# Top-k attention and SwiGLU FFN on one core: the order of V, scores and transposes on TensorE

## The chip, the cores and the metric

The kernel runs on one core of a Trainium2 chip. The metric is the time of one execution on the device in microseconds, as the median of several runs. The text names five engines as the profile does: PE (TensorE, matrix products and transposes; PEld is its loading of weights), DVE (VectorE), ACT (ScalarE), POOL (GpSimd) and SP (SyncE, which issues most DMAs).

## The reference

The inputs q, k and v have the shape 8 x 8 x 576 x 64 (batch, heads, sequence, head dimension), all in float32. Attention keeps for each query the 32 largest scores and gives all others no weight:

```python
scores = scale * np.matmul(q, k.transpose(0, 1, 3, 2))
kth = np.partition(scores, -top_k, axis=-1)[..., -top_k:-top_k + 1]
scores = np.where(scores >= kth, scores, -1000000000.0)
scores = scores - np.max(scores, axis=-1, keepdims=True)
attn = np.exp(scores)
attn = attn / (np.sum(attn, axis=-1, keepdims=True) + 1e-09)
x = np.matmul(attn, v)            # then (B,H,S,D) -> (B*S, H*D)
g = x @ w_gate                    # 512 x 1536
silu = g * (1.0 / (1.0 + np.exp(-g)))
out = (silu * (x @ w_val)) @ w_out   # 1536 x 512
```

There are 4608 tokens of 512 numbers after the attention.

## The kernel before

Heads are worked in pairs. A unit is one batch, one piece of the queries and one pair of heads. There are 160 units, counted n: for each of the 8 batches, four pieces of 128 queries (a full unit: two heads, 1152 scores a partition) and one last piece of 64 queries (a half unit, with both heads on the 128 partitions: 576 scores), for each of the four pairs. The four half units of a batch come together, at n mod 20 = 16 to 19.

The main loop (its body starts with `for n in range(NU + VALUES)`) is a pipeline that an iteration writes out by hand, and the order of writing is the order on each engine: at the end the kernel ties every instruction to the one before it on its engine. In iteration n stand, each for its own unit:

- `select(n)` on DVE: four rounds of MAX8 (L329) with MATCH_REPLACE8 (L333) between them find the 32 largest scores of each row of `sc`; then L339 writes a large negative number into `e` wherever a score is below the 32nd.
- `penalize(n - 1)` on POOL: L349 makes the bias, and L351 adds `sc` to `e`. This is the last reading of that unit's `sc`.
- `weigh(n - 1)` on ACT: exp with row sums (L360), and eps (L365).
- `normalize(n - 2)`: the reciprocal on DVE (L372), then a product on ACT (L375).
- `turn(n - 3)`, the transposes: `e` is transposed on PE (L387) in groups of four, one and four blocks (four and one for a half unit), and ACT copies each group to `et` (L388).
- `finish_unit(n - 4)` with `values`, called V here: the products with v on PE (L407 and L416) into one tile `av`, and ACT's copy to the FFN's input `xT` (L431).
- `scores(n + 1)`: a generator in two steps. The first issues the products of q and k on PE, four tiles `s` for a full unit (L308) and two for a half unit (L294). The second issues ACT's copies of these tiles to `sc` (L313, L299). `next(nxt)` runs the first step; `run(nxt)` runs what is left.

Every PSUM tile of the attention, those of the transposes, V, scores and of the preparation of k and q (`prep`, L255 and L263), comes from one pool of five banks, `ps_t`, in turn; the FFN has three banks of its own, `ps_f`. `sc` has two buffers, so the scores of n + 1 go into the buffer that unit n - 1 had.

Behind the attention's block of an iteration stand the FFN's pieces. `share(n)` and `credit` set how many an iteration gets. A block of 256 tokens (18 of them) starts once all V's of its tokens are written out: products with w_gate and w_val (L471), whose results ACT takes from PSUM (L496 to L498, L503) and POOL multiplies (L499, L504), then the products with w_out in a scheme of seven quarter products instead of eight (L557), with sums on POOL (L543 to L605). ACT's and POOL's parts of the FFN are kept in two lists, `on_act` and `on_pool`, and written out by `flush` at set places of the iteration.

In the first iterations the weights are loaded and rounded piece by piece as well (`rounded`, L114 to L123); `early[0]()` pulls ACT's part of one piece forward to its place between V's copy and exp. The loads of k, q and v are issued on SP after the block in question.

Of the kernel before, what the change touches and what calls it, by code (L numbers as in the profile page):

```python
# [25 lines left out]
def kernel(  # L26
# [174 lines left out]
    def rounding(n):  # L201
        for _ in range(n):
            next(weight, None)
# [28 lines left out]
    def load_v(i):  # L232
        b, hp = pairs[i]
        h = slice(2 * hp, 2 * hp + 2)
        vt = slabs.tile([P, 2, J, D], FP32, tag="v", name="v")
        v_last = slabs.tile([R, 2, D], FP32, tag="vl", name="v_last")
        vl = vlast[i % NV]
        nc.sync.dma_start(
            vt[:].rearrange("p h j d -> p h (j d)"),
            v[b, h, 0:JP].rearrange("h (p j) d -> p h (j d)", j=J),  # L240
        )
        nc.sync.dma_start(v_last[:], v[b, h, JP:S].rearrange("h p d -> p h d"))
        for hh in range(2):
            o = hh * R
            nc.sync.dma_start(vl[o : o + R, o : o + R], v[b, 2 * hp + hh, JP:S])
        vs[i] = (vt, v_last, vl)
# [27 lines left out]
    def n_heads(qt):  # L274

        return 1 if qt == J else 2

    def scores(n):
        b, qt, hp = units[n]
        slab = preps[b * NHP + hp]  # L280
        sc = work.tile([P, 2 * S], FP32, tag="sc", name="sc", bufs=2)
        halves = [slice(0, D), slice(D, P)]
        half = S // 2

        def bank():
            return ps_t.tile([P, 512], FP32, tag="t", name="s")


        if qt == J:
            banks = [bank() for _ in range(2)]  # L290
            for i, ps in enumerate(banks):
                for d in halves:
                    k0 = R + i * half
                    nc.tensor.matmul(  # L294
                        ps[d, 0:half], slab[d, S + R : S + 2 * R], slab[d, k0 : k0 + half]
                    )
            yield
            for i, ps in enumerate(banks):
                nc.scalar.copy(sc[:, i * half : (i + 1) * half], ps[:, 0:half])  # L299
        else:  # L300
            q0 = S + 2 * R + qt * P
            banks = []
            for i in range(2):
                for hh, d in enumerate(halves):
                    ps = bank()
                    banks.append((i + 2 * hh, ps))
                    k0 = (1 - hh) * R + i * half
                    nc.tensor.matmul(  # L308
                        ps[:, 0:half], slab[d, q0 : q0 + P], slab[d, k0 : k0 + half]
                    )  # L310
            yield
            for i, ps in banks:
                nc.scalar.copy(sc[:, i * half : (i + 1) * half], ps[:, 0:half])  # L313
        state[n] = dict(sc=sc)

    def select(n):

        nh = n_heads(units[n][1])
        sc = state[n]["sc"]
        m = small.tile([P, 2, TOP_K], FP32, tag="m", name="m", bufs=2)  # L320
        heads = [slice(t * S, (t + 1) * S) for t in range(nh)]
        rest = work.tile([P, 2 * S], FP32, tag="rest", name="rest", bufs=1)
        e = work.tile([P, 2 * S], FP32, tag="e", name="e", bufs=4)
        state[n] |= dict(m=m, e=e, heads=heads)
        cur = sc
        rounds = TOP_K // 8
        for r in range(rounds):
            for t, hs in enumerate(heads):
                nc.vector.max(m[:, t, 8 * r : 8 * r + 8], cur[:, hs])  # L329
                yield  # L330
            if r < rounds - 1:
                for t, hs in enumerate(heads):
                    nc.vector.match_replace(  # L333
                        rest[:, hs], m[:, t, 8 * r : 8 * r + 8], cur[:, hs], LOWEST
                    )
                    yield
                cur = rest
        for t, hs in enumerate(heads):
            nc.vector.tensor_scalar(  # L339
                e[:, hs], sc[:, hs], m[:, t, TOP_K - 1 : TOP_K], FAR, ALU.is_lt, ALU.mult  # L340
            )
# [26 lines left out]
    def normalize(n):  # L368
        st = state[n]
        tot, e, heads = st.pop("tot"), st["e"], st.pop("heads")  # L370
        nh = len(heads)
        nc.vector.reciprocal(tot[:, 0:nh], tot[:, 0:nh])  # L372
        yield
        for t, hs in enumerate(heads):
            nc.scalar.mul(e[:, hs], e[:, hs], tot[:, t : t + 1])  # L375
# [22 lines left out]
    def values(n):  # L398

        b, qt, hp = units[n]  # L400
        vt, v_last, vl = vs[b * NHP + hp]
        et = state.pop(n)["et"]
        last = qt == J
        ql = R if last else P
        av = ps_t.tile([P, P], FP32, tag="t", name="av")
        if not last:
            nc.tensor.matmul(av[:], vl[:], et[:, J, :], start=True, stop=False)  # L407
        for c in range(J + 1 if last else J):
            kl = R if c == J else P
            for hh in range(2):  # L410
                moving = (
                    et[0:kl, c, hh * R : (hh + 1) * R]
                    if last
                    else et[:, c + hh * (J + 1), :]
                )
                nc.tensor.matmul(  # L416
                    av[hh * R : (hh + 1) * R, 0:ql],
                    v_last[:, hh, :] if c == J else vt[:, hh, c, :],
                    moving,
                    start=last and c == 0,  # L420
                    stop=c == (J if last else J - 1),
                )
        c0 = b * S + qt * P
        at = c0
        while at < c0 + ql:
            kb = at // BLK
            n_c = min((kb + 1) * BLK, c0 + ql) - at
            if kb not in xT:
                xT[kb] = ffn.tile([P, NHP, BLK], FP32, tag="xT", name="xT", bufs=3)
                done[kb] = 0  # L430
            nc.scalar.copy(  # L431
                xT[kb][:, hp, at - kb * BLK : at - kb * BLK + n_c],
                av[:, at - c0 : at - c0 + n_c],
            )
            done[kb] += n_c
            at += n_c
# [16 lines left out]
    def flush(queue):  # L453
        while queue:
            queue.pop(0)()
# [224 lines left out]
    def fetch(n):  # L680

        b, qt, hp = units[n]
        i = b * NHP + hp
        if qt == 0:
            yield from prep(i)
        if qt == J and i + NHP < len(pairs):
            load(i + NHP)
# [19 lines left out]
    def run(steps):  # L707
        for _ in steps:
            pass

    def finish_unit(n):
        values(n)
        b, qt, hp = units[n]
        if qt == J and b + 1 < B:
            load_v((b + 1) * NHP + hp)
# [11 lines left out]
    TURN, VALUES = 3, 4  # L727
    due = [2.0]
    for n in range(NU + VALUES):
        nh = n_heads(units[n][1]) if n < NU else 1  # L730
        topk = select(n) if n < NU else no
        over[n - 1] = normalize(n - 1) if 0 <= n - 1 < NU else no
        nxt = scores(n + 1) if n + 1 < NU else no
        ahead = fetch(n + 2) if n + 2 < NU else no
        norm = over.pop(n - 2, no)

        def dve(k, beside=True):

            for _ in range(k * nh):
                next(topk, None)  # L740
                due[0] += 5 / 6 if beside else 0
                if due[0] >= 1:
                    due[0] -= 1
                    rounding(1)

        if n >= NU - NHP:
            credit[0] = 8.0
        else:
            credit[0] = min(credit[0] + share(n), share(n) + 1)
        flush(on_act)  # L750
        if 0 <= n - 1 < NU:
            penalize(n - 1)
        flush(on_pool)
        if 0 <= n - TURN < NU:
            run(turn(n - TURN))
        if n >= VALUES:
            finish_unit(n - VALUES)
        next(nxt, None)

        early[0]()  # L760
        if 0 <= n - 1 < NU:
            weigh(n - 1)
        run(nxt)


        dve(2, beside=False)
        if 2 <= n + 2 < NHP:
            load(n + 2)
        if n < NHP:
            load_v(n)  # L770
        pieces(2)
        flush(on_act)
        dve(1)
        dve(1)
        next(norm, None)
        run(norm)

        flush(on_pool)
        next(ahead, None)
        pieces(1)  # L780
        next(ahead, None)
        dve(1)
        pieces(1)
        dve(2, beside=False)
        run(topk)
        pieces(6)
# [50 lines left out]
```

## Time and profile before

| | |
|---|---|
| median of 3 runs | 1821.28 us (1821.05 to 1821.64) |
| span of the profiled execution, first to last instruction | 1817.8 us |
| between this span and the median of the runs | 3.5 us |
| mean granted clock of PE | 0.967 |
| busy: PE, DVE, ACT, POOL | 1708.7, 1610.7, 1218.7, 1036.4 us |
| ACT: exp (L360), both heads | 288 x 0.777 us |
| ACT: copies of scores (L313) | 512 x 0.402 us |
| ACT: copies of transposes (L388), large ones | 288 x 0.598 us |
| POOL: addition (L351), full unit | 128 x 2.640 us |

The profiled execution's time as a whole is not listed beside its span. Times in the profile count from the start of the span. A wait is listed as the engine and line that waited, what it waited for, and the time. A matmul's row is longer than the time until the next one can start, so a busy PE is not one at its peak; PE's speed is better seen in the starts of its rows.

### The profile page before, as it was taken

How to read it: one execution, taken by the hardware profiler on the slowest of the kernel's cores; microseconds unless marked ns; L12 is line 12 of the kernel's file. 1: busy time of each engine (PE TensorE's matmuls, PEld its weight loads, DVE VectorE, ACT ScalarE, POOL GpSimd, SP SyncE). 2: the span in 40 equal slices, each digit the busy share in tenths (PEclk: the TensorE clock that was granted, in tenths of full speed). 3: DMA queues.
4: the chain of work that ended last, by engine and by line, in shares of the span. 5: the costliest groups of instructions: out<-in, count | busy, mean ns of one | idle time of the engine just before them, and what ended most of it. 6: DMA issues, size and time to landing. Idle time of an engine off the chain costs nothing.

```text
span 1817.8 us, 30526 instructions
## 1 busy us (share of the span) xinstructions
PE 1708.7 (94%) x10756; PEld 1409.2 (78%) x10756; DVE 1610.7 (89%) x3372; ACT 1218.7 (67%) x2977; POOL 1036.4 (57%) x930
## 2 busy tenths in 40 slices
PE   4458999899999899999999999999999999999999
PEld 2346778687788788887888878887888878888887
DVE  7999999999999799997999989998999989998400
ACT  6778666676667676666767676767676766675532
POOL 5788756455565645554455636564556554646354
PEclk6669999899999999999999999999999999999999
DMA  7432030002100030000300021000300011000000
GB/s 191 125 108 90 14 85 7 12 1 50 45 1 13 2 82 12 13 1 22 73 12 2 13 56 39 1 12 3 74 19 13 1 36 33 1 13 12 1 12 12
DMA packets 109305, 59.65 MB, mean 33 GB/s; under 512 B 88544, under 2 KB 96992, under 8 KB 109152
## 3 DMA queue, kind: packets, MB, share of 16 engines
q1 hardware_dynamic: 108016, 57.37, 12.1%
q8 instruction: 85, 1.39, 0.3%
q14 instruction: 68, 0.56, 0.1%
q10 hardware_dynamic: 1136, 0.33, 0.1%
HBM read 48.23 MB, written 9.44 MB: 32 GB/s over the span
## 4 chain that ended last, share of the span: by engine, by line
PE 86%; DVE 8%; ACT 2%; POOL 2%; issue 2%; DMA 0%; SPq 0%; ACTq 0%; POOLq 0%
PE f L471 41%; PE x_ps L557 9%; PE av L416 8%; PE etps L387 7%; PE s L308 7%; PE y_ps L557 7%; DVE m L329 3%; DVE rest L333 3%; PE s L294 2%; PE av L407 1%; PE o_ps L517 1%; PE kqps L263 1%; DVE size L121 1%; DVE e L339 0%; POOL p L543 0%
## 5 line engine op out<-in xcount | busy, mean ns | idle before, releaser
L329 DVE MAX8 m<-rest 128x8 f32<-128x576 f32 x864 | 612.7, 744 | 2.2
L351 POOL TENSOR_TENSOR e<-e,sc 128x1152 f32<-128x1152 f32 (+1 forms) x160 | 383.1, 2394 | 83.7 <-DVE e L339 76.3
L333 DVE MATCH_REPLACE8 rest<-m,rest 128x576 f32<-128x576 f32 x576 | 423.1, 740 | 0.0
L471 PE MATMUL f<-xT,wg 128*128 128x256 f32 x1728 | 401.6, 382 | 0.0
L471 PE MATMUL f<-xT,wv 128*128 128x256 f32 x1728 | 399.1, 382 | 0.0
L471 PEld LDWEIGHTS f<-xT,wg 128*128 128x128 f32 x1728 | 323.1, 190 | 62.6 <-issue 21.3
L471 PEld LDWEIGHTS f<-xT,wv 128*128 128x128 f32 x1728 | 324.5, 190 | 58.7 <-issue 16.6
L499 POOL TENSOR_TENSOR h<-h,half_g 128x512 f32<-128x512 f32 x108 | 138.2, 1280 | 292.7 <-ACT h L498 292.2
L329 DVE MAX8 m<-sc 128x8 f32<-128x576 f32 x288 | 205.0, 747 | 104.0 <-ACT sc L299 57.8
L388 ACT COPY et<-etps 128x512 f32<-128x512 f32 (+1 forms) x448 | 184.1, 483 | 131.0 <-PE etps L387 130.2
L360 ACT ACTIVATE e<-e,bias 128x576 f32<-128x576 f32 x288 | 222.1, 777 | 57.5 <-POOL e L351 57.2
L387 PE MATMUL etps<-ident,e 128*128 128x128 f32 (+1 forms) x1312 | 184.5, 286 | 79.3 <-POOL size L122 18.2
L504 POOL TENSOR_TENSOR h<-h,val 128x512 f32<-128x512 f32 x108 | 139.6, 1293 | 186.3 <-ACT val L503 186.1
L387 PEld LDWEIGHTS etps<-ident,e 128*128 128x128 f32 (+1 forms) x1312 | 159.6, 147 | 106.0 <-POOL size L122 20.7
L375 ACT ACTIVATE e<-e,tot 128x576 f32<-128x576 f32 x288 | 212.0, 790 | 0.9 <-DVE tot L372 0.9
L333 DVE MATCH_REPLACE8 rest<-m,sc 128x576 f32<-128x576 f32 x288 | 211.5, 740 | 0.0
L308 PE MATMUL s<-kqT 64*128 64x288 f32 x1024 | 178.8, 449 | 14.1 <-ACT kqT L268 8.3
L339 DVE TENSOR_SCALAR e<-sc,m 128x576 f32<-128x576 f32 x288 | 177.2, 651 | 3.4
L416 PE MATMUL av<-et,v 128*64 128x128 f32 (+1 forms) x2560 | 170.3, 278 | 0.0
L313 ACT COPY sc<-s 128x288 f32<-128x288 f32 x512 | 164.0, 402 | 2.9 <-PE s L308 2.9
L496 ACT ACTIVATE h<-f 128x512 f32<-128x512 f32 x108 | 65.2, 604 | 133.3 <-PE f L471 133.3
L416 PEld LDWEIGHTS av<-et,v 128*64 128x64 f32 x2560 | 134.1, 143 | 22.8 <-issue 6.8
(73 smaller groups left out, 2029.1 us busy)
## 6 DMA issues: line engine op xcount, KB each, us to landing
v<-in_v_dram SPq DMA_DIRECT2D x32, 256.0 KB, 2.9
kq_in<-in_k_dram SPq DMA_DIRECT2D x63, 128.0 KB, 2.8
kq_in<-in_q_dram SPq DMA_DIRECT2D x63, 128.0 KB, 3.0
w<-in_moe_w_gate_dram SPq DMA_DIRECT2D x12, 512.0 KB, 3.7
w<-in_moe_w_val_dram SPq DMA_DIRECT2D x12, 512.0 KB, 3.8
w<-in_moe_w_out_dram SPq DMA_DIRECT2D x12, 512.0 KB, 3.5
out_dram<-o SPq DMA_DIRECT2D x38, 128.0 KB, 2.4
out_dram<-o SPq DMA_DIRECT2D x16, 256.0 KB, 2.4
```

The costliest lines, as they stand in the source:

```text
L308: nc.tensor.matmul(ps[:, 0:half], slab[d, q0 : q0 + P], slab[d, k0 : k0 + half])
L329: nc.vector.max(m[:, t, 8 * r : 8 * r + 8], cur[:, hs])
L333: nc.vector.match_replace(rest[:, hs], m[:, t, 8 * r : 8 * r + 8], cur[:, hs], LOWEST)
L339: nc.vector.tensor_scalar(e[:, hs], sc[:, hs], m[:, t, TOP_K - 1 : TOP_K], FAR, ALU.is_lt, ALU.mult)
L351: nc.gpsimd.tensor_tensor(e[:, every], e[:, every], sc[:, every], ALU.add)
L360: nc.scalar.activation(e[:, hs], e[:, hs], AF.Exp, bias=bias[:, t : t + 1], scale=scale, accum_out=tot[:, t : t + 1],)
L375: nc.scalar.mul(e[:, hs], e[:, hs], tot[:, t : t + 1])
L387: nc.tensor.transpose(ps[0:kl, c * P : (c + 1) * P], e[:, k0 : k0 + kl], ident[:])
L388: nc.scalar.copy(et[0:kl, c0 : c0 + cn, :], ps[0:kl, 0 : cn * P].rearrange("p (c j) -> p c j", c=cn),)
L416: nc.tensor.matmul(av[hh * R : (hh + 1) * R, 0:ql], v_last[:, hh, :] if c == J else vt[:, hh, c, :], moving, start=last and c == 0, stop=c ...
L471: nc.tensor.matmul(ps[:, i, :], w[:, kc, m * P : (m + 1) * P], x[:, kc, :], start=(kc == 0), stop=(kc == KC - 1),)
L557: nc.tensor.matmul(ps, lhsT, T[i][m], start=m == 0, stop=m == MQ - 1)
```

## The change

On PE, an iteration did the transposes of n - 3, V of n - 4 and the scores of n + 1. It now does V, scores and transposes. On ACT, the copies went transposes, V, (a piece of the weights), exp of n - 1, scores. They now go V, scores, transposes, (a piece of the weights), exp. To that end `run(nxt)`, which issues both steps of `scores`, stands where `next(nxt, None)` stood, and ahead of `turn`.

```diff
         if 0 <= n - 1 < NU:
             penalize(n - 1)
         flush(on_pool)
+        if n >= VALUES:
+            finish_unit(n - VALUES)
+        run(nxt)
         if 0 <= n - TURN < NU:
             run(turn(n - TURN))
-        if n >= VALUES:
-            finish_unit(n - VALUES)
-        next(nxt, None)
 
         early[0]()
         if 0 <= n - 1 < NU:
             weigh(n - 1)
-        run(nxt)
```

## The prediction

> **What bounds the kernel now.** I read the page first: shares of busy time, the slices and the chain.
>
> ```profile
> PE 1708.7 (94%) x10756; PEld 1409.2 (78%) x10756; DVE 1610.7 (89%) x3372; ACT 1218.7 (67%) x2977; POOL 1036.4 (57%) x930
> ...
> PE   4458999899999899999999999999999999999999
> ...
> PE 86%; DVE 8%; ACT 2%; POOL 2%; issue 2%; DMA 0%; SPq 0%; ACTq 0%; POOLq 0%
> ```
>
> TensorE is the bound from about 160 us on. In the first three slices it is half idle. Any wait put into TensorE's order after that moves the end; an earlier VectorE start does not. Next, the waits between 160 and 1750 us (engine and line, what it waited for, us in total, times, longest):
>
> ```profile
> ACT e L360 <- POOL e L351: 55.9, 30, 4.9
> ...
> DVE m L329 <- ACT sc L313: 36.7, 27, 2.2
> ...
> PE etps L387 <- issue: 12.4, 8, 3.6
> PE etps L387 <- ACT e L375: 9.9, 7, 4.6
> ```
>
> ScalarE waits 30 times for GpSimd's addition (L351) before it may take exp; VectorE waits for copied scores; TensorE waits hardly at all, 22.3 us before transposes. The third view is the timeline of one iteration, n = 129 (start, duration, engine, line):
>
> ```profile
> 1386.22 1.15 PE L387 MATMUL etps<-ident,e 128*128 128x128 f32 x9
> 1386.86 1.24 ACT L388 COPY et<-etps 128x512 f32<-128x512 f32 x3 [1.15 <-PE etps L387]
> 1387.21 0.39 PE L407 MATMUL av<-et,vlast 128*128 128x128 f32 x2
> 1387.52 1.09 PE L416 MATMUL av<-et,v 128*64 128x128 f32 x16
> 1388.55 1.24 PE L308 MATMUL s<-kqT 64*128 64x288 f32 x8
> 1388.66 0.27 ACT L431 COPY xT<-av 128x128 f32<-128x128 f32 x1 [0.56 <-PE av L416]
> 1389.72 1.56 PE L557 MATMUL y_ps<-wo,h 128*128 128x256 f32 x6
> 1390.76 2.65 POOL L351 TENSOR_TENSOR e<-e,sc 128x1152 f32<-128x1152 f32 x1
> 1393.44 0.78 ACT L360 ACTIVATE e<-e,bias 128x576 f32<-128x576 f32 x1 [4.51 <-POOL e L351]
> 1395.30 1.28 ACT L313 COPY sc<-s 128x288 f32<-128x288 f32 x4
> ```
>
> TensorE does transposes, V and scores in 3.5 us and goes on with the FFN at 1389.72, while ScalarE stands still until the addition ends at 1393.41. The scores wait in four PSUM banks, which TensorE does not need at that moment. That is the cover that the change touches.
>
> **The change part by part.** No instruction is added or removed and no DMA moves. Every load is issued after this block, and SP's and GpSimd's orders stay. The durations are those above.
>
> *TensorE's order.* The three groups take the same 3.5 us in any order: work 0. What changes is which banks they need. The pool `ps_t` turns over five banks. A full iteration takes V one, scores four, transposes three. In the new order the first transpose group falls on V's bank, the second and third on the banks of the first two scores. These come free when ScalarE has copied them (L313). That copy writes the `sc` buffer (two of them) which unit n-1 had, and GpSimd's addition for n-1 still reads it. So the second transpose group waits for that addition, and all FFN work stands behind it. Before, the wait fell on ScalarE alone.
>
> *Price of one such wait.* Call D the end of the addition less the start of TensorE's attention block. From the rows: V and scores take 2.4 us in issue (1387.21 to 1389.72 is 2.51), four transposes 0.44, so the third group could start 2.96 us in. Two copies take 0.77 with the handover. TensorE therefore stalls D - 2.2 us. For n = 129: D = 1393.41 - 1386.22 = 7.2, stall 5.0. The same from the waits view: ScalarE's wait plus 0.5.
>
> *Sum over the iterations after 160 us.* 55.9 us in 30 waits; four of them (2.7, 1.8, 4.7, 0.6) are where the next unit is a half unit: its scores take only two banks, and the transposes fall on banks freed earlier. 46.2 us are left, 26 waits, plus 26 x 0.5 = 59; with the iterations where ScalarE barely waited but D is 2.2 to 2.7, each iteration's own rows give 64.0. Two corrections. (a) Iterations at 1121, 1131, 1211, 1398 and 1409 us (3.0 + 1.1 + 0.9 + 2.6 + 1.0 = 8.6) follow a charged one: TensorE arrives there later by the stall before, and the addition, queued behind ScalarE's copies, hardly moves. (b) Around 161 to 200 and 347 to 385 us VectorE itself is late (12.1 us charged); there a stall repeats in iteration after iteration only on paper, since it uses up TensorE's lead, and TensorE already waited, up to 3.6 us at a time. I keep 4.6, minus 7.5. That leaves 47.9.
>
> *ScalarE's order.* Copies of transposes (1.24) now come behind the wait, so exp, normalisation (L375) and FFN copies run up to 1.24 us later after an addition. GpSimd's FFN products wait for those copies, and the next addition is queued behind the products. If every addition came 0.4 us later relative to TensorE the same sum would be 83, at 0.8 it is 106, at 0.5 us earlier 47. ScalarE idles before FFN copies for TensorE anyway (115.8 + 75.3 us in this window), so most of the lag is hidden: I take +6, ends -17 and +42. The FFN's own three banks don't run dry: at n = 129 TensorE did 6.6 us of FFN with none freed.
>
> *What it saves.* (c) TensorE's waits before transposes (22.3 us): V and scores now run first, 2.4 us of work, while the normalised e comes up to 1.24 us later; about 1 us each in ten waits, -10 (ends 0 and -22). (d) VectorE's 36.7 us of waits for scores mostly vanish, since the copies come about 3 us earlier. VectorE is off the path there, so 0. (e) Before 160 us TensorE is idle between units and VectorE 94% busy (149.75 of 160 us) with scores 6 us ahead of need: 0, with 5 either way for the weight rounding on ScalarE, which also moves behind the copies.
>
> *Clock.* After a long stall TensorE runs slower. Rows (10 us windows; the granted clock is the number after the POOL entry):
>
> ```profile
> 620.00:630.00 10.00, 10.00 (x67) 8.24 (x66) 5.76 (x12) 3.06 (x7) 7.48 (x11) 1.00 0.02 3
> 630.00:640.00 10.00, 5.38 (x36) 4.26 (x36) 5.18 (x11) 5.79 (x15) 4.46 (x5) 0.83 0.01 3
> ```
>
> A 4.6 us wait ended at 635.55 and the block after it took 5.1 us instead of 3.5, so 1.6 more; the same after a wait of 2.4 at 846.56 (5.2 us). Eight of my stalls are 2.5 us or longer: 8 x 1.6 = 13, minus the four slow blocks that the profile has already (6.5): +6. Ends 0 and +13. The Trainium skill, "TensorE: Matmul & The Clock Gate", section "HAM oscillation", speaks against this change too: it warns of TensorE idle gaps beyond about 3.4 us, after which work starts at half clock. By its threshold only the four stalls over 3.4 us would pay, and existing gaps nearly balance them, so its sum would be about 0 in place of +6. The trace's slow block after a 2.4 us wait is why I keep the rows' value.
>
> *Sum:* 47.9 + 6 - 10 + 0 + 6 = +50 us. The rows are from one profiled execution with a span of 1817.8 us; its time as a whole is not listed, and 3.5 us lie between that span and the median of the runs, 1821.28, which range over 0.6 us. I carry the 3.5 over: about 1870 us, 2.7% slower.
>
> **The rivals.**
> *A, the stall is mostly given back.* TensorE's lead is what makes D large; a stall eats the lead, and VectorE, no longer waiting for scores, runs ahead, so later additions end earlier. For: VectorE-late stretches behave so. Against: in most charged iterations GpSimd starts the addition 4 to 9 us after VectorE is done, behind FFN work that follows TensorE itself. Price: the sum at 0.5 us earlier, 47, less 16 for (a) and (b), less 22 for all transposes' waits: +9; up to +24 with half of these. 1830 to 1845.
> *B, faster.* If the addition is never later than 2.2 us into the block, the stalls are nil and (c) pays in full: 22 us, and half of VectorE-late stretches, up to 5: 1795 to 1810. It decides where D falls below 2.2 in all 44 iterations that exceed it; at n = 129 VectorE would have to pull GpSimd forward by 5 us, which it can't, because the products there wait for TensorE's sums. Speaking for it: 36.7 us of VectorE's waits go.
> *C, the lag feeds itself.* Copies late, products late, additions late, in most iterations: 106 to 135 by the sums at 0.8 and 1.24, less 16 and 10, plus 13: +93 to +122, about 1915 to 1945. Against: ScalarE's 191 us of waiting for FFN results.
> *D, the change doesn't do what it says:* the banks might not fall as counted, so that transposes do not wait; then the order is neutral, within 4 us.
>
> **How the numbers follow.** Forecast (1845 to 1905) 0.72, A 0.09, B 0.08, C 0.08, D 0.03. Time 1870, from the forecast alone. The range 1832 to 1905 holds the forecast and most of A, about 0.79. Its low end is the sum with A's bound and its high end the lag of 0.8 us (106 - 16 + 6 - 10 = +86). About 0.2%, 3.6 us, is what a measurement of this kernel can tell from no change: faster 0.08, same 0.03, slower 0.89.
>
> **What would show it.** Right: a new wait of transposes (L387) on ScalarE's score copies (L313, L299), some 40 to 60 us in 20 to 45 waits, longest about 5; the wait for L351 moved from exp to the score copies on ScalarE; VectorE's waits for L313 down to a third; granted clock below 0.967 on average; n = 129 with a gap of about 5 us between the transposes' first and second group. Wrong: if TensorE's waits before transposes stay under 25 us, the bank count or D's use failed (A, B, D); if many iterations stall by 1 to 2 us and GpSimd's additions shift, it is C. My weakest term is the lag, whose ends are 59 us apart.

## The result, and the profile after

The changed kernel takes 1869.28 us (median of 4 runs, 1867.31 to 1871.68) against 1821.16 us before. The ratio is 1.0264, with a 95% interval of 1.0249 to 1.0279: 48 us slower. The profiled execution took 1871.68 us as a whole, with a span of 1869.9 us, so 1.8 us lie around the span. The mean granted clock fell from 0.967 to 0.958.

The page of the profile after, in the same lines as before (shares of busy time, TensorE's slices, the chain by engine):

```profile
PE 1721.9 (92%) x10756; PEld 1413.7 (76%) x10756; DVE 1642.8 (88%) x3372; ACT 1218.5 (65%) x2977; POOL 1036.3 (55%) x930
...
PE   4558999799999999999999998999998999999999
...
PE 70%; DVE 10%; POOL 9%; ACT 9%; issue 1%; DMA 0%; SPq 0%; POOLq 0%; ACTq 0%; DVEq 0%
```

The counts of instructions are the same. The chain, which was TensorE's at 86%, now runs 16 points less through it; GpSimd and ScalarE, at 2% each before, have 9% each. Work that used to go on beside TensorE is now in its way.

The waits between 160 and 1800 us (engine and line, what it waited for, us in total, times, longest):

```profile
ACT sc L313 <- POOL e L351: 80.8, 38, 5.9
...
PEld etps L387 <- ACT sc L313: 59.2, 50, 5.1
...
PE etps L387 <- ACT sc L313: 48.8, 20, 4.9
...
DVE m L329 <- ACT sc L313: 47.8, 33, 5.1
...
ACT e L360 <- POOL e L351: 1.0, 1, 1.0
```

Two things are to be seen. ScalarE's wait for GpSimd's addition has left exp (55.9 us before, 1.0 now) and stands at the score copies. Behind it is a wait that did not exist before: TensorE's transposes wait for those copies, 48.8 us in 20 waits. The third view is the timeline of the same iteration as before, n = 129 (start, duration, engine, line):

```profile
1424.78 0.38 PE L407 MATMUL av<-et,vlast 128*128 128x128 f32 x2
1425.09 1.09 PE L416 MATMUL av<-et,v 128*64 128x128 f32 x16
...
1426.12 1.24 PE L308 MATMUL s<-kqT 64*128 64x288 f32 x8
...
1427.29 0.66 PE L387 MATMUL etps<-ident,e 128*128 128x128 f32 x4
...
1429.72 2.60 POOL L351 TENSOR_TENSOR e<-e,sc 128x1152 f32<-128x1152 f32 x1
1432.36 1.31 ACT L313 COPY sc<-s 128x288 f32<-128x288 f32 x4 [5.86 <-POOL e L351]
1432.81 1.42 PE L387 MATMUL etps<-ident,e 128*128 128x128 f32 x5 [4.87 <-ACT sc L313]
1433.53 1.33 ACT L388 COPY et<-etps 128x512 f32<-128x512 f32 x3
1434.02 2.62 PE L557 MATMUL y_ps<-wo,h 128*128 128x256 f32 x6
```

The first four transposes run at 1427.29, on V's bank. The other five start at 1432.81, right behind the first score copy, which itself came right behind the addition's end at 1432.32. The FFN's next six products, which took 1.56 us in this place before, take 2.62 us after the stall: the clock. A window around it:

```profile
1430.00:1440.00 10.00, 7.19 (x28) 6.14 (x29) 6.53 (x15) 5.99 (x15) 3.06 (x2) 0.83 0.00 0
```

Measured over all iterations by the starts of the transposes, 34 iterations after 160 us stall between the first and the second or third group, for 54.7 us in all (in each iteration the larger of the two gaps, beyond the pace; with both gaps 59.1 us). 20 of the stalls are over 0.5 us and hold 52.0 us. Before, such gaps came to 1.9 us.

### The profile page after: what moved, and what is told of

Same layout as the page of the kernel before. It is cut to its first block, busy times and chain, and to the rows that moved or that the text cites. A ratio compares the mean times of both kernels' runs of the same rounds, so it can differ in the third digit from the quotient of the medians.

```text
span 1869.9 us, 30657 instructions
## 1 busy us (share of the span) xinstructions
PE 1721.9 (92%) x10756; PEld 1413.7 (76%) x10756; DVE 1642.8 (88%) x3372; ACT 1218.5 (65%) x2977; POOL 1036.3 (55%) x930
## 4 chain that ended last, share of the span: by engine, by line
PE 70%; DVE 10%; POOL 9%; ACT 9%; issue 1%; DMA 0%; SPq 0%; POOLq 0%; ACTq 0%; DVEq 0%
PE f L471 37%; PE x_ps L557 8%; PE etps L387 7%; PE av L416 6%; PE s L308 5%; DVE m L329 4%; DVE rest L333 4%; POOL e L351 3%; PE y_ps L557 3%; ACT sc L313 2%; ACT e L360 2%; ACT et L388 2%; PE s L294 2%; POOL p L543 1%; POOL h L605 1%
## 5 line engine op out<-in xcount | busy, mean ns | idle before, releaser
L351 POOL TENSOR_TENSOR e<-e,sc 128x1152 f32<-128x1152 f32 (+1 forms) x160 | 383.1, 2394 | 57.5 <-DVE e L339 44.2
L471 PE MATMUL f<-xT,wv 128*128 128x256 f32 x1728 | 394.8, 379 | 0.0
L387 PE MATMUL etps<-ident,e 128*128 128x128 f32 (+1 forms) x1312 | 204.2, 295 | 106.9 <-ACT sc L313 61.5
L387 PEld LDWEIGHTS etps<-ident,e 128*128 128x128 f32 (+1 forms) x1312 | 148.3, 146 | 185.5 <-ACT sc L313 74.1
L313 ACT COPY sc<-s 128x288 f32<-128x288 f32 x512 | 167.4, 413 | 133.0 <-POOL e L351 98.3
L360 ACT ACTIVATE e<-e,bias 128x576 f32<-128x576 f32 x288 | 226.9, 810 | 1.0 <-POOL e L351 1.0
L339 DVE TENSOR_SCALAR e<-sc,m 128x576 f32<-128x576 f32 x288 | 206.9, 754 | 3.4
L375 ACT ACTIVATE e<-e,tot 128x576 f32<-128x576 f32 x288 | 208.4, 768 | 0.0
L388 ACT COPY et<-etps 128x512 f32<-128x512 f32 (+1 forms) x448 | 188.9, 515 | 4.5 <-PE etps L387 4.4
L308 PE MATMUL s<-kqT 64*128 64x288 f32 x1024 | 167.5, 446 | 23.0 <-ACT kqT L268 18.6
L431 ACT COPY xT<-av 128x128 f32<-128x128 f32 (+1 forms) x192 | 42.6, 239 | 196.0 <-PE av L416 195.9
```

The lines of the kernel that those rows point to most:

```text
L308: nc.tensor.matmul(ps[:, 0:half], slab[d, q0 : q0 + P], slab[d, k0 : k0 + half])
L339: nc.vector.tensor_scalar(e[:, hs], sc[:, hs], m[:, t, TOP_K - 1 : TOP_K], FAR, ALU.is_lt, ALU.mult)
L351: nc.gpsimd.tensor_tensor(e[:, every], e[:, every], sc[:, every], ALU.add)
L360: nc.scalar.activation(e[:, hs], e[:, hs], AF.Exp, bias=bias[:, t : t + 1], scale=scale, accum_out=tot[:, t : t + 1],)
L387: nc.tensor.transpose(ps[0:kl, c * P : (c + 1) * P], e[:, k0 : k0 + kl], ident[:])
L388: nc.scalar.copy(et[0:kl, c0 : c0 + cn, :], ps[0:kl, 0 : cn * P].rearrange("p (c j) -> p c j", c=cn),)
```

## The experiments

The theory: the wait for the addition (through the score buffer) holds PSUM banks that the transposes need, and TensorE, the bound, stands still. Its main rivals: the order costs by itself on ScalarE (exp and what follows run later), or on TensorE (the order of the matrix work). All times are compared with runs of the kernel before on the same chips, 1820.1 to 1821.5 us.

**1. ScalarE's part alone.** The score copies ahead of exp, TensorE's order unchanged:

```diff
-        next(nxt, None)
+        run(nxt)
...
             weigh(n - 1)
-        run(nxt)
```

> The kernel before, with only ScalarE's part moved by one step: the score copies stand ahead of the weights' piece and exp, but still behind the transposes' and V's copies; TensorE's order (transposes, V, scores) is that of before. Theory (the loss is TensorE's wait for PSUM banks that the waiting score copies hold): no transpose falls on a bank of this iteration's scores, so TensorE's waits for L313 stay under 10 us and the time within 8 us of before (1813 to 1829), with VectorE's waits for L313 at most as long as before's 36.7 us. Rival (ScalarE's new order costs by itself, since exp and the FFN copies behind it run later): 1835 to 1870, without such waits on TensorE.

Measured: 1831.11 us, ratio 1.0057 (1.0042 to 1.0072). The waits:

```profile
ACT sc L313 <- POOL e L351: 45.5, 22, 5.0
...
DVE m L329 <- ACT sc L313: 25.0, 23, 3.6
...
PE etps L387 <- ACT e L375: 13.2, 12, 4.4
```

No transpose waits for a score copy, as the theory has it, and three quarters of the loss are gone. But the time is 2 us outside what was expected: ScalarE's part costs about 11 us by itself. Gaps of over 0.6 us before transposes grew from 29.1 to 34.1 us (their waits for the normalised e, L375, from 10.9 to 13.2 us), and work lost at half clock from about 9 to 13 us (an estimate: half of the time at half clock after 165 us in which TensorE was at work). Those two make up some 9 of the 11 us. The rival is a small part, not the cause.

**2. The wait taken away from the copies.** The changed kernel, with an addition that does not read the scores (they are left out of exp):

```diff
-FAR = -3.0e38
+FAR = -1.0e38
...
-        nc.gpsimd.tensor_tensor(e[:, every], e[:, every], sc[:, every], ALU.add)
+        nc.gpsimd.tensor_tensor(e[:, every], e[:, every], e[:, every], ALU.add)
```

> The changed kernel, but GpSimd's addition (L351) reads the penalties twice instead of penalties and scores; it leaves the scores out of exp, and keeps its size and time. So the score copies no longer wait for GpSimd, only for VectorE's last reading of that buffer. Theory: the late additions are GpSimd's, not VectorE's, so nearly all of TensorE's 48.8 us of waits of transposes for L313 vanish (under 10 us stay, where VectorE itself is late) and the time comes to 1805 to 1828. Rival (the order of V, scores and transposes costs by itself, through clock, weight loads or ScalarE's lag): 1840 to 1870 with the waits gone.

Measured: 1795.09 us, ratio 0.986 (0.9843 to 0.9876). TensorE's waits of transposes for the copies fell to 2.6 us in one wait:

```profile
PE etps L387 <- ACT sc L313: 2.6, 1, 2.6
```

The time is 10 us below what was expected: the order not only costs nothing by itself, it is worth some 25 us. Whether leaving the scores out had a part in that was open until experiment 5.

**3. The addition earlier in GpSimd's order.** The changed kernel with

```diff
-        if 0 <= n - 1 < NU:
-            penalize(n - 1)
         flush(on_pool)
...
         run(topk)
+        if n < NU:
+            penalize(n)
         pieces(6)
```

> The changed kernel, with the bias and addition of unit n (L349, L351) written out at the end of iteration n, ahead of its last FFN pieces, instead of at the start of iteration n + 1 behind them. Nothing is left out. Theory (the addition is late because GpSimd does FFN sums queued ahead of it): the additions end 2 us or more earlier in most of the iterations charged, TensorE's waits for L313 fall from 48.8 to 5 to 25 us and the time to 1815 to 1845. Rival (the addition is late because of VectorE, or GpSimd has no free time earlier): waits and time stay, 1860 to 1875; or FFN sums that now stand behind the addition hold TensorE up instead, with new waits for L543 to L605.

Measured: 1833.01 us, ratio 1.0069 (1.0054 to 1.0084), 36 us less than the changed kernel, with TensorE's waits for L313 at

```profile
PE etps L387 <- ACT sc L313: 28.4, 13, 4.3
```

The time is as expected; the waits are not: 28.4 us lie just outside the 5 to 25. GpSimd's order makes part of the additions late, not most of them. Of the 20 stalls over 0.5 us 8 are gone, among them those of the iterations that lay at 1109 and 1386 us before, and 12 are left. In nine of these twelve GpSimd still began the addition 4 to 10 us after VectorE was done: at 736 and 1013 us (stalls of 2.6 and 4.5 us) 9 and 10 us after, behind FFN sums that had themselves waited for ScalarE's copies. In the other three VectorE itself was late. The 36 us are about 23 us of TensorE's waits and, by the same estimate as in experiment 1, 13 us of work that is no longer lost at half clock.

**4. The transposes behind two FFN pieces.** The changed kernel with

```diff
         run(nxt)
-        if 0 <= n - TURN < NU:
-            run(turn(n - TURN))
...
         pieces(2)
+        if 0 <= n - TURN < NU:
+            run(turn(n - TURN))
         flush(on_act)
```

> The changed kernel, with the transposes and their copies moved behind the iteration's first two FFN pieces: TensorE does V, scores, two pieces (about 3.4 us), transposes. Nothing is left out. Theory (a stall is the addition's end less 2.2 us less whatever stands between): stalls are left only where D is over about 5.6 us, some 5 us in all, and TensorE's former waits before transposes stay gone: 1808 to 1832. Rival (transposes late make V and the FFN late, or ScalarE's copies behind the pieces pile up): 1840 to 1870, with new waits of V (L407, L416) for L388 or of the FFN for its banks.

Measured: 1850.95 us, ratio 1.0163 (1.0148 to 1.0179): a miss, and the rival's range. TensorE's waits:

```profile
PE etps L387 <- ACT sc L313: 17.4, 12, 3.0
PE av L407 <- ACT et L388: 16.9, 17, 4.3
PE s L308 <- ACT kqT L268: 11.1, 14, 1.4
...
ACT sc L313 <- POOL e L351: 127.4, 68, 6.6
```

The FFN work does cover the wait (48.8 us down to 17.4), but the additions come later as well: ScalarE waited for them 127.4 us in 68 waits at L313, against 80.8 in 38, and D, the addition's end less the start of the attention block, is 2.5 us in the mean instead of 1.6. And V of the next iteration now waits for the copies of transposes that were done so late. Covering a wait by moving the waiter made the next one.

**5. A third score buffer,** with the new order and with the old one. Room for it is made by using e as the scratch of the search:

```diff
-        sc = work.tile([P, 2 * S], FP32, tag="sc", name="sc", bufs=2)
+        sc = work.tile([P, 2 * S], FP32, tag="sc", name="sc", bufs=3)
...
-        rest = work.tile([P, 2 * S], FP32, tag="rest", name="rest", bufs=1)
         e = work.tile([P, 2 * S], FP32, tag="e", name="e", bufs=4)
+        rest = e
```

> The changed kernel with three score buffers instead of two; the room comes from letting the rounds of the search for the 32 largest use e as their scratch in place of a tile of their own. Nothing is left out, and the number of instructions is the same. The copies for n + 1 now wait for GpSimd's addition of n - 2, which ended an iteration ago. Theory: TensorE's waits of transposes for L313 all but vanish (under 5 us) and the time is that of the run without scores in the addition, 1795, or up to 10 us more if VectorE must wait for transposes before it may write e so early: 1790 to 1810. Rival (leaving the scores out of exp was what made that run fast): 1840 to 1870.

> The kernel before with the same third score buffer and e as scratch. There the score copies stand behind exp on ScalarE, which waits for the same addition anyhow. Theory (buffers matter only together with the new order): 1813 to 1825. Rival (the buffer alone is the gain): 1790 to 1805.

Measured with the new order: 1795.46 us, ratio 0.9863 (0.9848 to 0.9878). With the old order: 1822.37 us, ratio 1.001 (1.0 to 1.0019). That is a square of four: two buffers 1821 (old order) and 1869 (new), three buffers 1822 and 1795. The buffer is worth nothing in the old order and 74 us in the new one; the order costs 48 us with two buffers and gains 27 with three (25 against the kernel before on the same chip). The edit also makes e the scratch; that this is not the gain is seen in the old order, where it is worth nothing, and in experiment 2, which reached the same 1795 us without it. Leaving the scores out in experiment 2 had no part in its time either. No wait of transposes for score copies is left on TensorE. The waits with the new order and three buffers:

```profile
ACT e L360 <- POOL e L351: 28.5, 19, 3.2
...
DVE m L329 <- ACT sc L313: 3.3, 8, 0.7
```

The wait for the addition is back at exp, where TensorE does not care; VectorE's waits for full units' scores are down to 3.3 us.

**6. V alone moved ahead.** From the kernel before:

```diff
-        if 0 <= n - TURN < NU:
-            run(turn(n - TURN))
         if n >= VALUES:
             finish_unit(n - VALUES)
+        if 0 <= n - TURN < NU:
+            run(turn(n - TURN))
         next(nxt, None)
```

> The kernel before with V alone moved ahead of the transposes: TensorE does V, transposes, scores, and ScalarE copies V, transposes, (weights' piece), exp, scores. No transpose falls on a bank of this iteration's scores, and no copy is moved in front of the addition. Theory: V's 1.2 us of work run while the transposes wait for the normalised e, so TensorE's 23.3 us of waits before transposes after 160 us fall by about half: 1805 to 1818. Rival (the gain of the new order comes from the early scores alone): 1818 to 1824.

Measured: 1827.45 us, ratio 1.0041 (1.0026 to 1.0056), outside both expectations. The waits before transposes did fall by half:

```profile
PE etps L387 <- ACT e L375: 9.5, 4, 3.4
PE kqps L255 <- ACT sc L313: 2.5, 2, 1.4
PE etps L387 <- issue: 1.3, 2, 1.2
```

10.8 us in place of 23.3. But the block of attention work itself grew. From the start of the last FFN product ahead of it to the start of the fourth product behind it takes 4.461 us in the order transposes, V, scores (median of the 77 blocks after 160 us in which all three units are full and four FFN products follow), 4.610 us as V, transposes, scores, and 4.414 us as V, scores, transposes. 0.149 us in some 134 blocks is 20 us more, less 12.5 us of waits: +7.5 by this estimate, and +7.3 was measured. Two smaller terms cancel: block 12 starts 2.7 us later, and 2.7 us less work is lost at half clock.

**7. Exp ahead of the transposes' copies.** In the changed kernel, `turn` is split into its transposes, which stay, and its copies, which go behind `weigh`:

```diff
-            run(turn(n - TURN))
+            turned = turn(n - TURN)
+            next(turned)
...
             weigh(n - 1)
+        if 0 <= n - TURN < NU:
+            run(turned)
```

> The changed kernel, but ScalarE copies V, scores, then does the weights' piece and exp, and copies the transposes last; TensorE's order stays and its transposes need the same banks. Exp so runs 1.24 us earlier after an addition, the transposes' copies 2 us later. Theory: TensorE's waits for L313 stay within 10 us of the changed kernel's 48.8, and if the lag of exp and normalisation behind the copies costs what was charged (6 us), the time falls by 2 to 10 us: 1859 to 1869. Rival (the lag is a large part of the loss): 1820 to 1850, with the additions ending 0.5 us or more earlier in most charged iterations.

Measured: 1873.79 us, ratio 1.0292 (1.0277 to 1.0308), outside both expectations. TensorE's waits (this kernel's lines from `turn` on have numbers 2 to 4 higher):

```profile
PE etps L389 <- ACT sc L313: 46.2, 21, 4.9
PE av L409 <- ACT et L392: 10.8, 5, 4.1
```

The stalls stay, and V waits 10.8 us for late copies, against 3.4 us. Exp earlier does not help; what its lag costs by itself this run does not show, since the late copies cost as well, but it is not where the 48 us are.

**8. Three more combinations.** First the kernel before with both the early score copies of experiment 1 and the third buffer:

> The kernel before with the score copies ahead of exp (as in the first experiment) and the third score buffer: ScalarE copies transposes, V, scores, then does the weights' piece and exp; TensorE's order is that of before. Nothing is left out. Theory (the gain of the new order is TensorE's: V and scores cover the wait for the normalised e, and the block of 36 matrix instructions is 0.05 us shorter): the copies no longer wait, the 11 us that they cost with two buffers mostly go, and the time is that of before, 1814 to 1826. Rival (the early scores are the gain): 1793 to 1806.

Measured: 1824.24 us, ratio 1.0016 (1.0007 to 1.0025). Early scores alone are no gain even when nothing holds them; the gain is in TensorE's order. Then the third buffer and the new order, with the addition earlier as in experiment 3:

> The changed kernel with the third score buffer and, besides, the addition written out ahead of the iteration's last FFN pieces. Nothing is left out. Theory: with three buffers no wait for the addition is left on TensorE's path, so an earlier addition is worth little: 1788 to 1800, ScalarE's wait for L351 (28.5 us with the third buffer alone) at most half. Rival (GpSimd's FFN sums, now behind the addition, come late for TensorE's products): 1800 to 1815, with longer waits of L557 for GpSimd.

Measured: 1794.34 us, ratio 0.9847 (0.9831 to 0.9864), ScalarE's wait for L351 at 13.6 us: the same time as with the third buffer alone, whose own interval it overlaps. Last, the kernel before with the addition earlier and nothing else:

> The kernel before with only the addition written out ahead of the iteration's last FFN pieces. Nothing is left out. Theory (before, ScalarE's 55.9 us of waits for the addition cost almost nothing, because TensorE does FFN work meanwhile): ScalarE's waits for L351 fall to 10 to 30 us and the time by 0 to 8 us: 1812 to 1821. Rival (those waits, through exp and the normalised e, cause TensorE's waits before transposes): 1795 to 1810, with these waits halved.

Measured: 1813.6 us, ratio 0.9964 (0.9951 to 0.9977). ScalarE's waits at exp and the gaps before the transposes:

```profile
ACT e L360 <- POOL e L351: 24.3, 15, 3.4
...
PE etps L387 <- ACT e L375: 6.3, 7, 2.0
```

Exp's wait falls by 31.6 us and the time by 8, most of it through shorter waits before transposes (gaps over 0.6 us: 23.2 instead of 29.1 us). The clock has no part in it: the profiled execution's mean is 0.978, but after 165 us it was at half clock for 23.5 us, as before the change, and the other four executions, with means of 0.965 to 0.968, took the same time within 2 us. The 55.9 us that looked free before were nearly so, and not quite.

## Why the prediction was right, step by step

The time was 1870 predicted and 1869.28 measured, +50 against +48. The mechanism held in its links: the bank, the buffer behind it, the addition behind that, and, for part of the additions, GpSimd's queue in front (experiment 3). Experiment 5's two runs with three buffers show that without this wait the change does not cost but gains. That the sum came within 2 us is partly luck, as the terms show. (The range's ends differ by 2 us from their own sums: 9 and 86 us above 1821 are 1830 and 1907, where 1832 and 1905 stand.)

*The price of one wait, D - 2.2 us.* At n = 129 after the change, D is 1432.32 - 1424.78 = 7.5, so the rule gives 5.3; the two groups of transposes stand 5.0 us further apart than their pace. Right, if 0.3 us high; it is so in most of the larger stalls (n = 93: 4.8 against 4.4).

*The sum of stalls, 47.9 and 6 for the lag.* 53.9 predicted, 54.7 measured (59.1 with both gaps of each iteration). Correction (a) holds: of the five iterations that follow a charged one, two stall, by 1.0 and 1.2 us, in place of the 8.6 us that were left out. For (b), at 161 to 200 and 347 to 385 us, 4.6 was kept and 6.5 measured. The lag is not general. Over the 44 iterations charged, D moved by 0.04 us in the median, while it rose in a few: from 3.48 to 6.39 at n = 29, from 5.65 to 6.95 at n = 93, from 4.42 to 5.53 at n = 139. All in all the part of D above 2.2 us rose from 64.0 to 69.5 us, near the 6 that were charged.

*Waits saved (c), -10.* TensorE's 22.3 us before transposes (23.3 up to 1800 us, the window after the change) became 1.8 us behind L375 and issue and 1.6 behind V's copy (L431), but 9.7 us came back as V waiting for L388 (3.4) and scores waiting for the prepared k and q (6.3). 23.3 - 13.1 is 10.2. Right.

*VectorE (d).* The expected sign, waits for L313 down to a third, failed: they rose from 36.7 to 47.8 us. The copies were expected 3 us earlier, but with two buffers they cannot pass the addition: 28 of the 47.8 us are seven waits that end about 1.1 us behind copies that had themselves waited 1.8 to 5.9 us for it. The waits fell to 3.3 us only with the new order and the third buffer. That this term is worth 0 in time was right: experiment 8's first run shortens them to 16.7 us and gains nothing.

*The first 160 us (e).* Iteration 12's block starts 1.4 us later than before, within the 5 either way.

*The clock, +6: mis-sized.* The trace's clock records show 23.5 us at half clock after 165 us before the change, 56.7 us after it, and 11.6 us with the third buffer. Half of the time at half clock is lost work, less where TensorE stood still anyway: 25.0 us after against 9.3 us before, 16 us more. The slow block after a stall was rightly priced at 1.6 us where it lasts 3.4 us, but 12 stalls set it off, not eight, and after four of them it lasted 6.8 us. (In the side sum by the threshold of 3.4 us, only two of the four slow blocks that the profile had already follow a wait longer than that, 3.6 and 4.6 us, so it would have been about +3, not 0.)

*TensorE's order, 0: mis-sized the other way.* The new order saves 0.047 us a block, 134 blocks, 6 us.

*The sum.* The two profiled executions' spans differ by 52.1 us. TensorE's waits (what gaps over 0.6 us between two starts exceed 0.2 us by, after 160 us) rose by 38.4, from 31.0 to 69.4; predicted were 47.9 + 6 - 10 = 43.9. Work lost at half clock rose by 16, predicted 6. The order saved 6 and the first 160 us cost 1.4, both put at 0. That is 50 us in all, with 2 us not assigned: the clock's error and those of the waits and the order nearly cancel, so the sum is closer than its terms.

*The gain of the order without the stalls* was put at 22 us for rival B and came to 25 (three buffers, against the kernel before): 6 us from the block, 8 us from waits (31.0 to 23.2, counted as above), about 5 from the clock; 6 us are not assigned. Rival B's price came near, but only the 8 us are what it was made of, and its condition was wrong: D need not fall if there is a third buffer. Of rival A, stalls given back by TensorE's lost lead, only the follow-on iterations show anything. Rival C did not come: the lag did not feed itself. Rival D fell with the first wait of L387 for L313.

## What to carry to other kernels

When work moves forward in an engine's order, ask for each tile in a rotating pool which earlier tile must be let go for it, and follow that release through every queue until the last waiter; a wait that was free on a slack engine becomes the bound's wait if it holds what the bound needs. Price it from the trace before the change: the end of the late work less the time at which the bound would get there, iteration by iteration, and leave out iterations that a stall just before has already shifted. A reordering that loses may lack only one buffer: run it with that buffer and run the old order with it, since only the four times together tell the order's worth from the buffer's.

## What the runs showed of the hardware

The order of three groups of matrix work changed its length without any wait: 4.461, 4.610 and 4.414 us for the orders named in experiment 6, the same 35 instructions. The difference lies where groups meet, as the starts of iteration 127 show in the traces of before, experiment 6 and after. Behind the scores (64-row products) the next group's first instruction starts 0.33 us after the last of them, before as after the change. The second one then follows after 0.319 us if it is an FFN product, whose steady pace is 0.216 us, but after 0.165 us if it is a transpose, whose pace is 0.109 us: 0.10 us over the pace against 0.06. Behind the transposes the first two FFN products come after 0.109 and 0.218 us. V starts 0.109 us behind the transposes, while the transposes behind V come after 0.203 and 0.166 us, which with the scores 0.203 us behind the transposes makes V, transposes, scores the longest order. Why, no run tells.

Short stalls set off the half clock as well, and their length alone does not decide. In the kernel before, a wait of 2.4 us ahead of 846.56 us was followed by 3.4 us at half clock, while one of 2.1 us (by the starts around it) ahead of 340 us was not. After the change a wait of 1.6 us ahead of 192.78 us was followed by it, and one of 2.5 us ahead of 1707.03 us was not. The Trainium skill, "TensorE: Matmul & The Clock Gate", section "HAM oscillation", sets the limit at idle gaps of about 3.4 us; in these runs the clock also fell after shorter ones, so the measured row is the better price.
